# One scheduling priority for every exponential of the scores in a four-layer linear-attention and memory-attention kernel

## The chip, the cores and the metric

The kernel runs on one core of a Trainium2 chip. The metric is the device time of one execution in microseconds (us); the time before is the median of three runs. The engines are named as in the profile: PE is TensorE (PEld its weight loads), DVE is VectorE, ACT is ScalarE, POOL is GpSimd, SP is SyncE, which only issues DMA transfers. L1068 is line 1068 of the kernel.

## The reference

Four layers in the order A, B, A, B on an input of 2048 rows by 640; each adds its result to its input. `H` = 32 heads of 20.

```python
# A: linear attention
qkv = (layernorm(x) @ wqkv) split into q, k, v;  phi(t) = where(t > 0, t + 1, exp(t)) + 1e-6
pq, pk = phi(q), phi(k)
o = (pq @ (pk.T @ v)) / (pq @ sum(pk) + 1e-6);   x = x + o @ wo
# B: memory and local attention over 4 segments of 512 rows
for s in range(4):
    p = softmax(qs @ ks.T * scale + causal mask)
    a_mem = (phi(qs) @ M) / (phi(qs) @ z + 1e-6)          # phi without the 1e-6
    o = sigmoid(beta) * a_mem + (1 - sigmoid(beta)) * (p @ vs)
    M, z = M + phi(ks).T @ vs, z + sum(phi(ks))
x = x + concat(o) @ wo
```

## The kernel before

**Two streams.** The kernel is written as two generators. The *dense* stream holds all projections, the layernorms, the linear attention of the A layers, and the memory and output of the B layers. The *attention* stream holds the causal softmax of the two B layers. `run` weaves them: it steps the stream that has the smaller estimated cost so far. What comes out is the written order. TensorE takes its instructions exactly in that order (`manual_schedule` for PE). For ScalarE, VectorE, GpSimd and SyncE a scheduler decides when the kernel is built: of the instructions that it takes to be ready it picks by priority, which is the place in the written order, moved forward by `tc.high_priority(offset=n)` for what is written inside that block. Once built, each engine's order is fixed.

**Attention.** A B layer has 4 segments of 8 groups of 4 heads, so there are 64 groups in all. Each goes through `attention` in three stretches (the table `STRETCHES`; the third number of an entry says how many groups back it works, so that three groups are under way at a time):

- `row_max`: scores with the queries as rows (TensorE, L1023) and their row maxima (VectorE, L1029); `split_max` (VectorE, L1038 and L1039) and `max_rows` (L1047 to L1052) turn the maxima into two more rows of the queries.
- `scores`: the scores again, transposed, with the maximum taken off by the matmul (L1064) into one PSUM bank; the exponential by ScalarE (L1068) into a tile `pe`, of which there are ten; the selection of the causal part of a diagonal block by GpSimd (L1075). A group has ten banks, written as five pairs by `EXPS[0]` to `EXPS[4]`: 640 exponentials and 640 selections.
- `weigh` (TensorE, L1091) multiplies the exponentials by the values, `evacuate` (ScalarE, L1097) and `normalize` (L1104 to L1115) finish the group.

**PSUM.** All PSUM tiles come from one pool of eight banks. Which instruction reads a bank last (an exponential, or one of the dense instructions below) decides when TensorE may write into it again; the banks are handed on in the order in which they come free.

**Dense instructions near the exponentials.** `turn` (L325 to L339) transposes a 128-row tile by TensorE (L332) in two parts of three and two chunks; ScalarE writes the upper half of each number, in 16 bits (L336), and VectorE the lower half from that (L337). The projection that reads both, `proj_n`, issues for each of the five chunks three matmuls (L415): upper by upper, upper by the weight's lower half, and lower by upper. `proj_t` (L400) does the same for queries and keys, whose result goes through `split_store` (L853 by ScalarE, L854 by VectorE, then a store). `phi` (B layers: L439 exponential `e`, L441 relu `r`, both ScalarE, L442 VectorE) and `phi_a` (A layers: L429, L431, L432) make phi, reading the same PSUM bank twice. In B layers L442 makes `pkT`, which TensorE turns (L881) and ScalarE writes out (L883) for `update`: L891 TensorE, L897 VectorE, which adds to `acc`; at a segment's end the memory `mem` is added up by VectorE (L750). `normed` (L387, ScalarE) makes a layernorm's row `xh`. `o_half` writes half of an output tile (L491 ScalarE, L492 GpSimd), and `b_out` stores it (L990, issued by ScalarE).

Of the kernel before, what the change touches and what calls it, by code (L numbers as in the profile page):

```python
# [144 lines left out]
class Kernel:  # L145
# [974 lines left out]
    def attention(self, segs):  # L1120

        prev = old = ahead = None
        n = 0
        while n < NSEG * NG or prev or old:
            new = None
            if n < NSEG * NG:
                st = segs[n // NG]
                if not st.get("projected"):
                    yield lambda: st.get("projected")
                new = ahead or self.stacks(st, n % NG)  # L1130
                ahead = None
            n += 1
            for stretch in STRETCHES:
                for op, k, back in stretch:
                    G = (new, prev, old)[back]
                    if op == "load" and n < NSEG * NG and segs[n // NG].get("projected"):
                        if prev:
                            with self.tc.issue_after(self.rowed.ins):
                                ahead = self.stacks(segs[n // NG], n % NG)
                        else:  # L1140
                            ahead = self.stacks(segs[n // NG], n % NG)
                    if G is None:
                        continue
                    if op == "max":
                        self.row_max(G, MAXES[k])
                    elif op == "split":
                        self.split_max(G)
                    elif op == "rows":
                        self.max_rows(G)
                    elif op == "exp":  # L1150
                        with self.tc.high_priority(offset=200) if k == 4 else nullcontext():
                            for bank in EXPS[k]:
                                self.scores(G, bank)
                    elif op == "sum":
                        self.weigh(G, k)
                    elif op == "copy":
                        self.evacuate(G)
                    elif op == "out":
                        if not G["st"].get("remembered"):
                            yield lambda: G["st"].get("remembered")  # L1160
                        self.normalize(G)
                yield SLOT
            old, prev = prev, new
# [244 lines left out]
```

## Time and profile before

| | |
|---|---|
| Three runs, median (lowest to highest) | 1684.12 us (1683.84 to 1685.31) |
| Profiled execution: time, span | 1683.68 us, 1681.9 us |
| Time outside the span | 1.78 us |
| Granted TensorE clock, mean | 0.997 |
| TensorE busy (weight loads) | 1625.1 us (1018.3 us) |
| VectorE, ScalarE, GpSimd busy | 1262.9, 994.8, 505.5 us |
| First and last exponential of scores | 363.7 us, 1654.2 us |

The span is the time from the first to the last instruction of the profiled execution. A timeline's line gives the start, the length, the engine, the line in the kernel, what it writes and reads, how many instructions it stands for ("x4"), and in brackets how long the engine stood idle before it and what ended that. Starts and lengths of several instructions on one line are those of the first start and the total. In a view of who waits, a line gives the engine and line that waited or was waited for, the microseconds, and the number of times.

### The profile page before, as it was taken

How to read it: one execution, taken by the hardware profiler on the slowest of the kernel's cores; microseconds unless marked ns; L12 is line 12 of the kernel's file. 1: busy time of each engine (PE TensorE's matmuls, PEld its weight loads, DVE VectorE, ACT ScalarE, POOL GpSimd, SP SyncE). 2: the span in 40 equal slices, each digit the busy share in tenths (PEclk: the TensorE clock that was granted, in tenths of full speed). 3: DMA queues.
4: the chain of work that ended last, by engine and by line, in shares of the span. 5: the costliest groups of instructions: out<-in, count | busy, mean ns of one | idle time of the engine just before them, and what ended most of it. 6: DMA issues, size and time to landing. Idle time of an engine off the chain costs nothing.

```text
span 1681.9 us, 37873 instructions
## 1 busy us (share of the span) xinstructions
PE 1625.1 (97%) x13818; PEld 1018.3 (61%) x13818; DVE 1262.9 (75%) x4015; ACT 994.8 (59%) x1888; POOL 505.5 (30%) x1046
## 2 busy tenths in 40 slices
PE   8999998999999999999999999999999999999999
PEld 6767766564475566556556777765546645645555
DVE  6788796397887788759874465947888888878773
ACT  5665553346757746667666464333675676676674
POOL 3442141113223332333351210310322332232452
PEclk9999999999999999999999999999999999999999
DMA  6415546331322332362211303534233323323432
GB/s 221 149 56 192 215 168 205 124 113 58 113 80 70 117 127 67 125 194 75 84 45 41 118 32 108 185 100 135 68 109 102 107 88 111 112 84 104 143 102 95
DMA packets 110514, 190.98 MB, mean 114 GB/s; under 512 B 14188, under 2 KB 69868, under 8 KB 107768
## 3 DMA queue, kind: packets, MB, share of 16 engines
q1 hardware_dynamic: 97704, 142.68, 26.3%
q0 software_dynamic: 3264, 24.91, 4.2%
q10 hardware_dynamic: 9360, 20.98, 3.2%
q8 instruction: 109, 1.79, 0.4%
q14 instruction: 77, 0.63, 0.1%
HBM read 109.32 MB, written 78.64 MB: 112 GB/s over the span
## 4 chain that ended last, share of the span: by engine, by line
PE 72%; DVE 14%; ACT 8%; DMA 3%; issue 2%; SPq 1%; POOL 1%; ACTq 0%; DVEq 0%; POOLq 0%
PE ps L415 30%; PE ps L400 13%; PE ps L1091 8%; PE ps L591 5%; PE ps L1064 4%; PE ps L332 4%; PE ps L1023 3%; ACT pe L1068 3%; DVE ps L1029 2%; PE ps L468 2%; PE ps L1104 1%; DVE e L432 1%; DVE wmx L245 1%; DVE nat L854 1%; DVE pk L554 1%
## 5 line engine op out<-in xcount | busy, mean ns | idle before, releaser
L1029 DVE CUSTOM_DVE_ANT_0 ps<-ps,maskw 128x384 f32<-128x384 f32 (+3 forms) x1024 | 472.7, 520 | 32.3 <-PE ps L1023 28.1
L1068 ACT ACTIVATE pe<-ps,lsc 128x512 f32<-128x512 f32 x640 | 394.8, 695 | 83.3 <-PE ps L1064 67.9
L1075 POOL TENSOR_SCALAR_AFFINE_SELECT pe<-pe 128x256 f32<-128x256 f32 (+1 forms) x640 | 230.9, 367 | 397.6 <-ACT pe L1068 394.4
L415 PEld LDWEIGHTS <-xT 128*128 128x128 f16 x2880 | 280.7, 98 | 110.5 <-issue 4.5
L415 PEld LDWEIGHTS <-oT 128*128 128x128 f16 x1920 | 185.3, 98 | 87.3 <-issue 7.8
L1091 PE MATMUL ps<-pe,v 128*32 128x512 f32 (+3 forms) x2048 | 157.2, 436 | 9.8 <-POOL pe L1075 3.3
L415 PE MATMUL ps<-wm,oT 128*128 128x320 f16 x960 | 142.7, 301 | 4.8 <-DVE oT L337 4.4
L415 PE MATMUL ps<-w_Bo,oT 128*128 128x320 f16 x960 | 141.5, 299 | 3.8 <-ACT oT L336 2.0
L1029 DVE DVE_READ_ACCUMULATOR2_ANT mg<- 128x1 f32 x1024 | 143.8, 140 | 0.1
L591 PE MATMUL ps<-pk,xs 128*128 128x321 f16 (+1 forms) x960 | 139.0, 302 | 5.0 <-DVE pk L554 2.4
L400 PE MATMUL ps<-xT,w_Bq 128*128 128x512 f16 x600 | 140.9, 380 | 1.3 <-ACT pe L1068 0.8
L415 PE MATMUL ps<-w_Ak,xT 128*128 128x320 f16 x960 | 139.7, 301 | 1.6 <-DVE xT L337 0.9
L400 PE MATMUL ps<-xT,w_Bk 128*128 128x512 f16 x600 | 138.5, 379 | 1.2 <-ACT pe L1068 1.2
L415 PE MATMUL ps<-w_Bv,xT 128*128 128x320 f16 x960 | 139.3, 299 | 0.1
L415 PE MATMUL ps<-w_Aq,xT 128*128 128x320 f16 x960 | 137.6, 299 | 0.0
L1064 PE MATMUL ps<-qs,ks 62*128 62x512 f16 (+3 forms) x1024 | 129.5, 299 | 3.6 <-ACT pe L1068 2.2
L591 PEld LDWEIGHTS <-xs 128*128 128x128 f16 x960 | 93.4, 98 | 44.9 <-DVE pk L554 2.8
L1023 PE MATMUL ps<-ks,qs 60*128 60x512 f16 (+3 forms) x1024 | 115.8, 297 | 2.3 <-ACT pe L1068 1.1
L432 DVE SCALAR_TENSOR_TENSOR e<-e,r 128x320 f32<-128x320 f32 x128 | 68.2, 534 | 63.7 <-ACT r L431 63.1
L854 DVE SCALAR_TENSOR_TENSOR nat<-ps,nat 128x512 f16<-128x512 f32 x80 | 55.2, 690 | 66.2 <-ACT nat L853 65.8
L1091 PEld LDWEIGHTS ps<-pe,v 128*32 128x32 f32 x2048 | 63.2, 109 | 68.9 <-issue 47.3
L336 ACT ACTIVATE oT<-ps 128x384 f16<-128x384 f32 (+1 forms) x128 | 55.9, 445 | 71.7 <-PE ps L332 54.3
(202 smaller groups left out, 2369.0 us busy)
## 6 DMA issues: line engine op xcount, KB each, us to landing
x<-xn ACTq DMA_DIRECT2D x48, 320.0 KB
qs<-qd SPq DMA_DIRECT2D x128, 120.0 KB
ks<-kd SPq DMA_DIRECT2D x128, 120.0 KB
xo<-x SPq DMA_DIRECT2D x48, 320.0 KB
pqi<-pqd SPq DMA_DIRECT2D x32, 320.0 KB
qd<-nat SPq DMA_DIRECT2D x40, 256.0 KB
kd<-nat SPq DMA_DIRECT2D x40, 256.0 KB
x<-in_A_x SPq DMA_DIRECT2D x16, 320.0 KB
```

What stands on the lines that cost most here:

```text
L332: nc.tensor.transpose(pt[:, (c - c0) * P:(c - c0 + 1) * P], src[:, c * P:(c + 1) * P], self.ident)
L400: nc.tensor.matmul(p, w[:, c, a, t * P:(t + 1) * P], xT[:, c, b, :], start=k == 0, stop=k == 3 * C - 1)
L415: nc.tensor.matmul(p, xT[:, c, a, i * P:(i + 1) * P], w[:, c, b, n * HN:(n + 1) * HN], start=k == 0, stop=k == 3 * C - 1)
L432: nc.vector.scalar_tensor_tensor(e, e, 1.0, r, op0=OP.min, op1=OP.add)
L591: nc.tensor.matmul(p, xs[:, i, a, c * P:(c + 1) * P], pk[i][:, b, cols], start=i == 0 and a == b, stop=i == NT - 1 and a == 1)
L854: nc.vector.scalar_tensor_tensor(nat[:, 1], p, QK_SHIFT, nat[:, 0], op0=OP.mult, op1=OP.subtract)
L1023: nc.tensor.matmul(bs[par][:, a:a + n], qs[r, p, i * P:(i + 1) * P], ks[r, p, :n], start=True, stop=True)
L1029: nc.vector.tensor_tensor_reduce(bs[par][:, a:a + n], bs[par][:, a:a + n], self.maskw[:, SEG - n:], 1.0, NEG, OP.add, OP.max, G["mg"][:, p ...
L1064: nc.tensor.matmul(b[:, a:a + n], ks[r, p, j * P:(j + 1) * P], qs[r, p, j * P:], start=True, stop=True)
L1068: nc.scalar.activation(e, b, AF.Exp, scale=self.lsc)
L1075: nc.gpsimd.affine_select(d, d, pattern=pat, compare_op=OP.is_ge, fill=0.0, base=0, channel_multiplier=-1)
L1091: nc.tensor.matmul(G["pv"][32 * h4:32 * h4 + 32, j * P:], v[j][:, h * E1:h * E1 + 32], G.pop((p, par, j)), start=j == 0, stop=j == 2, skip ...
```

## The change

Before, only the last pair of a group (`EXPS[4]`) was written at a priority 200 places ahead, and the other four pairs at none. Now these four have a priority 100 places ahead; the last pair keeps its 200. The block holds all of `scores`: on TensorE it decides nothing (that order is the written one), on ScalarE and GpSimd it moves exponentials and selections against the dense instructions.

```diff
                     elif op == "exp":
-                        with self.tc.high_priority(offset=200) if k == 4 else nullcontext():
+                        with self.tc.high_priority(offset=200 if k == 4 else 100):
                             for bank in EXPS[k]:
                                 self.scores(G, bank)
```

No instruction is added or removed. The orders of TensorE and SyncE are the same before and after. On ScalarE 90 of the 640 exponentials stand earlier, in 32 places, each time ahead of one or two dense instructions: 12 places (25 exponentials) pass e and r of `phi` (L439, L441), 8 (24) pass `xh` (L387), 7 (25) pass r of `phi_a` (L431, at some also L567), 2 (5) pass L491, 2 (8) pass L336, and 1 (3) passes the issue of a store (L990). On GpSimd nine selections stand earlier. On VectorE, which has no instruction inside the block, some 27 dense instructions stand later, because what they read now comes later.

Three places follow. First ScalarE near the end, in the last segment of the last B layer (1625 us in the trace of before). `oT` are the halves that the output projection reads, `xn` an output row. Before:

```order
L491 ACTIVATE xn<-ps,ioB 128x320
L1068 ACTIVATE pe<-ps,lsc 128x512
L990 DMA out_x<-xn 128x640
L1068 ACTIVATE pe<-ps,lsc 128x512 x3
L336 ACTIVATE oT<-ps 128x3x128
L336 ACTIVATE oT<-ps 128x2x128
L1068 ACTIVATE pe<-ps,lsc 128x512 x4
L336 ACTIVATE oT<-ps 128x3x128
L491 ACTIVATE xn<-ps,ioB 128x320
```

Now:

```order
L491 ACTIVATE xn<-ps,ioB 128x320
L1068 ACTIVATE pe<-ps,lsc 128x512
L990 DMA out_x<-xn 128x640
L1068 ACTIVATE pe<-ps,lsc 128x512 x7
L336 ACTIVATE oT<-ps 128x3x128
L336 ACTIVATE oT<-ps 128x2x128
L336 ACTIVATE oT<-ps 128x3x128
L491 ACTIVATE xn<-ps,ioB 128x320
```

The four exponentials that followed the first two `oT` instructions now stand before them.

Second VectorE at the end of the second B layer's third segment (1403 us). `pkT` is phi of the keys, `m_19613` the split row maxima, `mem_80` the segment's memory. Before:

```order
L897 TENSOR_TENSOR acc<-ps,acc 128x63
L442 SCALAR_TENSOR_TENSOR pkT<-e,r 128x512
L1038 TENSOR_SCALAR m_19613<-mg 128x2x8
L750 TENSOR_TENSOR mem_80<-acc,blk 32x3x63
L1039 SCALAR_TENSOR_TENSOR m_19613<-mg,m_19613 128x2x8
L750 TENSOR_TENSOR mem_80<-acc,blk 32x3x63 x2
L750 TENSOR_TENSOR mem_80<-acc,blk 32x63
L854 SCALAR_TENSOR_TENSOR nat<-ps,nat 128x512
```

Now:

```order
L897 TENSOR_TENSOR acc<-ps,acc 128x63
L1038 TENSOR_SCALAR m_19613<-mg 128x2x8
L750 TENSOR_TENSOR mem_80<-acc,blk 32x3x63
L1039 SCALAR_TENSOR_TENSOR m_19613<-mg,m_19613 128x2x8
L750 TENSOR_TENSOR mem_80<-acc,blk 32x3x63 x2
L750 TENSOR_TENSOR mem_80<-acc,blk 32x63
L442 SCALAR_TENSOR_TENSOR pkT<-e,r 128x512
L854 SCALAR_TENSOR_TENSOR nat<-ps,nat 128x512
```

`pkT` now stands behind the maxima's split and the memory. (On ScalarE at this place, its e and r stand behind two exponentials that followed them.)

Third ScalarE in the first B layer, where `phi_a` of the next A layer's queries is made (783 us). Numbers behind names tell tiles apart. Before:

```order
L336 ACTIVATE oT_10927<-ps_10928 128x3x128
L429 ACTIVATE e_10950<-ps_10934,inv_Aq_601 128x320
L431 ACTIVATE r_10952<-ps_10934,inv_Aq_601 128x320
L1068 ACTIVATE pe_10960<-ps_10957,lsc_2933 128x512
L1068 ACTIVATE pe_10966<-ps_10963,lsc_2933 128x512
L1068 ACTIVATE pe_10985<-ps_10982,lsc_2933 128x512
L1068 ACTIVATE pe_10991<-ps_10988,lsc_2933 128x512
L336 ACTIVATE oT_10927<-ps_11000 128x2x128
```

Now:

```order
L336 ACTIVATE oT_10927<-ps_10928 128x3x128
L429 ACTIVATE e_10950<-ps_10934,inv_Aq_601 128x320
L1068 ACTIVATE pe_10960<-ps_10957,lsc_2933 128x512
L1068 ACTIVATE pe_10966<-ps_10963,lsc_2933 128x512
L1068 ACTIVATE pe_10985<-ps_10982,lsc_2933 128x512
L1068 ACTIVATE pe_10991<-ps_10988,lsc_2933 128x512
L431 ACTIVATE r_10952<-ps_10934,inv_Aq_601 128x320
L336 ACTIVATE oT_10927<-ps_11000 128x2x128
```

`r_10952`, the second reader of the bank `ps_10934`, now stands behind four exponentials.

## The prediction

> **What bounds the kernel now.** I read the page first, then the groups by line, then everything that stands around the exponentials (L1068), then the timeline wherever the change moves one.
>
> ```profile
> span 1681.9 us, 37873 instructions
> PE 1625.1 (97%) x13818; PEld 1018.3 (61%) x13818; DVE 1262.9 (75%) x4015; ACT 994.8 (59%) x1888; POOL 505.5 (30%) x1046
> PE 72%; DVE 14%; ACT 8%; DMA 3%; issue 2%; SPq 1%; POOL 1%; ACTq 0%; DVEq 0%; POOLq 0%
> L1068 ACT ACTIVATE pe<-ps,lsc 128x512 f32<-128x512 f32 x640 | 394.8, 695 | 83.3 <-PE ps L1064 67.9
> ```
>
> TensorE is busy for 1625.1 of 1681.9 us, and its order is the written one, which the change leaves alone. So only the 56.8 us in which it stands can shrink, and whatever makes it stand longer adds. ScalarE is busy 59% of the span: it is no bound, but it serves TensorE in turn, and the change alters whose turn comes first. One exponential has 695 ns. Who waits for exponentials is told by the view of line 1068:
>
> ```profile
>   POOL pe L1075: 394.4, 429
>   PE ps L1091: 2.4, 6
>   PE ps L891: 2.4, 6
>   PE ps L1064: 2.2, 6
>   PE ps L400: 2.0, 5
>   PE ps L1023: 1.1, 3
>   PE ps L415: 0.6, 2
>   PE ps L332: 0.6, 2
> ```
>
> GpSimd waits for them for 394.4 us, but it is busy 30% of the time and bounds nothing. TensorE waits 2.4+2.4+2.2+2.0+1.1+0.6+0.6 = 11.3 us, in 30 instances, for all 640. Nearly all are waits for a PSUM bank (all eight are in one pool, so the exponential that reads a bank frees it for whatever TensorE does next). 11.3 us is therefore all that earlier exponentials could ever bring, if nothing else became later.
>
> **What the change moves.** TensorE's and SyncE's orders stay. On ScalarE 90 of the 640 exponentials, in 32 places, go ahead of one or two dense instructions; on GpSimd nine selections move; on VectorE some 27 dense instructions slip behind maxima and memory updates. No instruction is added or removed. So the cost is that of the passed dense instructions, place by place: what each feeds, and when that is wanted.
>
> *The oT halves, two places.* The first is in the last B segment, at 1625 us:
>
> ```profile
> 1625.19 0.77 ACT L336 ACTIVATE oT<-ps 128x384 f16<-128x384 f32 x2
> 1625.36 0.37 PE L1064 MATMUL ps<-qs,ks 62*128 62x384 f16 x2 [0.20 <-ACT pe L1068]
> 1625.72 0.89 DVE L337 TENSOR_TENSOR oT<-ps,oT 128x384 f16<-128x384 f32 x2
> 1625.82 2.45 ACT L1068 ACTIVATE pe<-ps,lsc 128x512 f32<-128x512 f32 x4
> 1626.42 0.52 PE L332 MATMUL ps<-ident,otok 128*128 128x128 f32 x3 [0.69 <-DVE oT L337]
> 1626.78 2.20 PE L415 MATMUL ps<-w_Bo,oT 128*128 128x320 f16 x15
> 1628.10 0.55 ACT L336 ACTIVATE oT<-ps 128x384 f16<-128x384 f32 x1
> 1628.74 0.56 DVE L337 TENSOR_TENSOR oT<-ps,oT 128x384 f16<-128x384 f32 x1 [0.85 <-ACT oT L336]
> ```
>
> Here ScalarE makes the upper halves of oT (L336), VectorE the lower ones (L337), and the output projection (L415) reads both: its third matmul is the first that needs a lower half. The four exponentials now run first. Their slot is 2.28 us (1625.82 to the next instruction at 1628.10), and their scores are done by 1625.36+0.37 = 1625.73 at the latest, in time for the third and fourth. So the first L336 starts at 1625.19+2.28 = 1627.47 and not at 1625.19. VectorE follows 0.53 behind its start (1625.72 against 1625.19) and takes 0.56: the lower half is there at 1628.56, and with 0.06 for the handover the third matmul starts at 1628.62. Before, it started two steps of 2.20/15 = 0.147 after 1626.78, at 1627.07. That is **+1.55 us**. Bounds: no less than 0 (it would have to be absorbed by a later wait), no more than the whole slot, 2.28. The L332 before it waited 0.69 for VectorE to free a bank and now gets one from the first exponential, but the projection behind it still waits, so this brings nothing.
>
> The second such place is at 1573.86, and what it turns is read by the projection that begins here:
>
> ```profile
> 1579.89 0.31 PE L415 MATMUL ps<-w_Bo,oT 128*128 128x320 f16 x1
> ```
>
> A delay of 2.28 us disappears in the six before that. Without that cover it would cost as much as the first.
>
> *e and r in front of pkT, 12 places, 25 exponentials* (L439, L441). The two are pushed back by two exponentials, 1.14 us. In eleven places what they feed is wanted later. The twelfth is the segment's last tile:
>
> ```profile
> 1402.27 0.70 ACT L439 ACTIVATE e<-ps,inv_Bk 128x512 f32<-128x512 f32 x1
> 1403.36 0.22 DVE L897 TENSOR_TENSOR acc<-ps,acc 128x63 f32<-128x63 f32 x1
> 1403.41 1.29 ACT L1068 ACTIVATE pe<-ps,lsc 128x512 f32<-128x512 f32 x2
> 1403.58 0.69 DVE L442 SCALAR_TENSOR_TENSOR pkT<-e,r 128x512 f32<-128x512 f32 x1
> 1404.19 0.17 DVE L1038 TENSOR_SCALAR m<-mg 128x16 f16<-128x16 f32 x1
> 1404.90 1.13 DVE L750 TENSOR_TENSOR mem<-acc,blk 32x189 f32<-32x189 f32 x3
> 1405.12 0.60 PE L881 MATMUL ps<-ident,pkT 128*128 128x128 f32 x4
> ```
>
> The push of 1.14 is the distance of ScalarE's starts, 1402.27 to 1403.41. VectorE pays more than that, since pkT's place in its order is now behind L1038, L1039 and all of L750. Those last from 1404.19 to 1404.90+1.13 = 1406.03, 1.84 us; begun at 1403.58 they end at 1405.42, and pkT at 1406.11 instead of 1404.27. The transposes L881 began at 1405.12, behind TensorE's own earlier work, and now begin at about 1406.16: **+1.04 us**. Least: 0.3, if VectorE took pkT as soon as r is there (1403.58+1.14+0.69 = 1405.41). Most: 1.84, if TensorE had been held to pkT already. For the other eleven I take 0, because what frees the last bank of the group is finished when all four instructions are, in either order:
>
> ```profile
> 540.14 0.75 ACT L441 ACTIVATE r<-ps,inv_Bq 128x512 f32<-128x512 f32 x1
> 542.19 0.64 PE L1091 MATMUL ps<-pe,v 128*32 128x512 f32 x4 [0.30 <-ACT pe L1068]
> ```
>
> Here the matmul waited 0.30 for the last exponential and will wait as long for r. Bounds: 0.75 against 0.695 a place, +0.6 in all; or this 0.30 gone wherever it stands, which the gains below hold.
>
> *r of the linear layers, seven places, 25 exponentials* (L431):
>
> ```profile
> 782.94 0.38 PE L1064 MATMUL ps<-qs,ks 62*128 62x384 f16 x4
> 783.02 0.52 ACT L431 ACTIVATE r<-ps,inv_Aq 128x320 f32<-128x320 f32 x1
> 783.43 2.42 ACT L1068 ACTIVATE pe<-ps,lsc 128x512 f32<-128x512 f32 x4
> 783.59 2.20 PE L415 MATMUL ps<-w_Ak,xT 128*128 128x320 f16 x15
> ```
>
> At 783.59 TensorE starts as r ends (783.54) and frees its bank. Now an exponential stands there, which takes 0.695 and not 0.52: +0.17. Five of the seven have this shape: **+0.85 us** (0 to 1.2, seven places). r itself is four exponentials late, 2.28 us; it goes through VectorE into a store whose result no matmul of this stretch reads. If it were read at once, seven places would cost 16 us.
>
> *xh of the layernorm, eight places, 24 exponentials* (L387):
>
> ```profile
> 476.27 0.91 ACT L387 ACTIVATE xh<-xn,nb,rs 128x640 f32<-128x640 f32 x1
> 489.57 0.60 PE L332 MATMUL ps<-ident,xh 128*128 128x128 f32 x4
> ```
>
> xh comes three exponentials later, 3 x 0.57 = 1.7 us, and is turned 12 us after it was made: 0. Without that cover it would be 1.7 each, 14 us. The last three places (L491 twice, an output store once) pass work with no reader near: 0.
>
> *Gains.* The 90 moved exponentials end sooner. If the 11.3 us were spread evenly over 640, those outside the e/r places (65) would hold 65/640 x 11.3 = 1.1; the timeline shows some waits of 0.1 to 0.2 at them, and I take **-1.0 us** (bounds 0 and 90/640 x 11.3 = 1.6).
>
> Sum: 1.55+1.04+0.85-1.0 = **+2.4 us**. The profiled execution took 1683.68 us, 0.44 below the median of 1684.12, and 1.78 outside its span. The edit touches nothing outside the span, so 1683.68 becomes 1686.1, and the median 1686.5.
>
> **A rule against the change.** ScalarE's own waits for scores are in the list of waits:
>
> ```profile
> ACT pe L1068 <- PE ps L1064: 67.9, 80, 3.5
> ```
>
> Eighty of the 640 exponentials stood on ScalarE until their scores came, 67.9/80 = 0.85 us each, 3.5 the longest. Whatever stands behind such a one waits too, and a moved exponential has ready dense work behind it. At the places above the scores end before the slot (1625.73 for the last one at 1625; at 783 the slot is 783.02, and the matmuls of the second pair begin at 782.94, so the first pair is through), so my sum holds nothing for it. [...]
>
> **Rivals.** *Slower: the moved exponential blocks.* If the 32 places met unfinished scores as often as the rest (80 of 640), four would, for 0.85 each: 3.4 us on top, if TensorE waits behind each. That is 1686.5+3.4 = 1689.9; with the two holes at their upper bounds alone (0.73 and 0.8 more) 1688.0. It decides once 1.0 us is added to my sum, so from two such places. Against it: where I followed the scores, they were done. Chance 0.22.
>
> *Slower: the clock.* The two holes widen TensorE's idle time, and the granted clock is not full in every stretch (columns: TensorE busy first, the clock is the third value from the right):
>
> ```profile
> 240.00:300.00 60.00, 54.37 (x436) 38.32 (x434) 42.77 (x107) 21.67 (x50) 14.70 (x18) 0.97 0.51 176
> 1620.00:1680.00 60.00, 56.47 (x477) 36.05 (x475) 27.95 (x89) 30.90 (x60) 20.50 (x42) 1.00 0.30 100
> ```
>
> With 5.6 us idle in 60 the clock was 0.97; with 3.5 us it was 1.00. The last stretch gets 1.55 more, 5.1, close to the former. Price: 0.03 x 60 = 1.8 us, 1688.3. [...] No row here shows the step itself. Chance 0.06.
>
> *No change: nothing shows.* 550 exponentials stay where they were, and the holes may be taken up by waits that follow them. Then only small gains and losses remain: 1684.1, at the lowest 1684.12-1.6 = 1682.5. Against it: TensorE stood only 3.5 us in the last 60, mostly for its own results. Chance 0.14.
>
> *Faster: freed banks run ahead.* Thirty waits for exponentials against 32 places. If half the 11.3 us went and no hole appeared, 1684.1-5.6 = 1678.5. It would decide from 3.4 us on. Against it: the places are where the scheduler had a choice, not where TensorE waited, and the 0.30 above doesn't go. Chance 0.08.
>
> **The numbers.** The forecast has 0.50, from 1685.1 to 1687.4. 0.2% is 3.4 us, about what a measurement can tell from no change: 1680.7 to 1687.5. Same: forecast and no change, 0.64; slower: 0.22+0.06 = 0.28; faster 0.08. The range goes from the lowest of the no-change case, 1682.5, to 1689.5, and leaves out the faster case and the top of the first rival, some 0.15.
>
> **What would show it.** Right: at about 1626.4 TensorE stands some 1.6 us ahead of an L415 released by VectorE's L337; at about 1405 some 1.0 us ahead of L881, released by L442; its busy time stays 1625; its waits for L1068 stay between 9 and 12 us. Wrong: neither hole there, an L1068 in front of which ScalarE idles at a moved place while TensorE stands, waits for L1068 below 8, or a clock under 1.00 in the last 60 us.

## The result, and the profile after

| | before | after |
|---|---|---|
| Median of 20 runs each (lowest to highest) | 1683.78 us (1680.32 to 1686.06) | 1685.83 us (1683.27 to 1688.28) |
| Ratio of the runs, 95% interval | | 1.0015 (1.0009 to 1.0022) |
| Profiled execution: time, span | 1683.68, 1681.9 us | 1685.54, 1683.8 us |
| Granted TensorE clock in it | 0.997 | 0.995 |

The change costs 1.5 to 3.7 us. The page of the profile after:

```profile
span 1683.8 us, 37888 instructions
PE 1625.1 (97%) x13818; PEld 1018.1 (60%) x13818; DVE 1260.8 (75%) x4015; ACT 995.1 (59%) x1888; POOL 503.6 (30%) x1046
```

TensorE's busy time has the same sum as before, 1625.1 us, but differences offset in it: with its instructions matched one to one (below), it is busy 3.1 us longer from 1624 us on, most of that at half clock, 1.5 us shorter ahead of the first exponential of scores, and 1.6 us shorter between. So the 1.9 us of the span can't be read as waiting alone. Who waits for exponentials, from the view of line 1068 after:

```profile
  PE ps L1064: 2.8, 7
  PE ps L891: 2.4, 6
  PE ps L1091: 2.2, 3
  PE ps L400: 2.0, 5
  PE ps L1023: 1.1, 3
  PE ps L332: 0.8, 3
  PE ps L415: 0.6, 2
```

That is 11.9 us where it was 11.3: ninety exponentials earlier, and TensorE waits for exponentials no less. What it waits for otherwise is seen at the two places of the prediction. The timeline after, at 1625 us:

```profile
1625.16 1.19 ACT L336 ACTIVATE oT<-ps 128x384 f16<-128x384 f32 x3
1625.72 1.35 DVE L337 TENSOR_TENSOR oT<-ps,oT 128x384 f16<-128x384 f32 x3 [1.01 <-ACT oT L336]
1625.75 4.24 PE L415 MATMUL ps<-w_Bo,oT 128*128 128x320 f16 x15 [1.57 <-ACT oT L336]
1629.92 0.61 PE L1064 MATMUL ps<-qs,ks 62*128 62x256 f16 x4
```

The projection stands 1.57 us for oT's upper half. But then its fifteen matmuls take 4.24 us, where they took 2.20 before. The stretches of the same kernel show why (the clock is the third value from the right):

```profile
1624.00:1626.00 2.00, 0.43 (x4) 0.13 (x2) 0.92 (x5) 2.00 (x6) 1.33 (x4) 0.58 0.05 17
1626.00:1628.00 2.00, 2.00 (x9) 0.97 (x8) 1.08 (x3) 0.35 (x1) 0.00 (x0) 0.50 0.00 0
1628.00:1630.00 2.00, 2.00 (x10) 0.91 (x10) 0.00 (x0) 0.00 (x0) 0.00 (x0) 0.50 0.00 0
1630.00:1632.00 2.00, 2.00 (x18) 0.80 (x22) 1.01 (x3) 1.79 (x3) 1.22 (x2) 0.71 0.00 0
1620.00:1680.00 60.00, 56.79 (x458) 35.00 (x455) 26.22 (x83) 30.49 (x59) 20.28 (x42) 0.94 0.27 91
```

The clock of 0.58 in the first row means half speed from about 1624.3 on, while TensorE stands (1624.18 to 1625.75); the trace's records of the clock put the spell at 1624.32 to 1631.15. So behind the wait TensorE works at half speed for 5.4 us; over the 60 us the clock is 0.94, where it was 1.00. The other place, after:

```profile
1403.67 0.69 DVE L442 SCALAR_TENSOR_TENSOR pkT<-e,r 128x512 f32<-128x512 f32 x1
1404.42 0.66 PE L881 MATMUL ps<-ident,pkT 128*128 128x128 f32 x4 [0.76 <-DVE pkT L442]
```

L881 had no wait before and has 0.76 now, for VectorE's L442, as forecast (some 1.0).

Since TensorE's order is the same in both kernels, its instructions can be matched one to one, and the difference of their starts (after less before) tells where time was lost. Up to the first exponential both kernels are the same; that one started 1.2 us sooner in the profile after, by chance (over the profiles shown below this start scatters by 2 us to either side). Counted from there, in us:

| stretch of before | step | what is there |
|---|---|---|
| 364 to 782 | -0.35 | several small ones |
| 782 to 833 | +0.24 | r places (L431) |
| 833 to 850 | +0.47 | L1091 waits 1.40, not 0.70 |
| 862 to 868 | -0.85 | L591 no longer waits for L611 |
| 868 to 1395 | +0.07 | |
| 1395 to 1409 | +0.97 | L881 waits for L442 |
| 1558 to 1564 | -0.99 | the issue of a store is short |
| 1588 to 1592 | -0.56 | L415 waits 0.24, not 0.81, for L336 |
| 1624 to 1631 | +3.89 | the wait for oT and the half clock |
| 1631 to the end | +0.28 | |

The rest of -0.1 lies between 1409 and 1558; the sum is +3.06. What makes the +0.28 behind 1631 was not followed.

### The profile page after: what moved, and what is told of

Same layout as the page of the kernel before. It is cut to its first block, busy times and chain, and to the rows that moved or that the text cites. A ratio compares the mean times of both kernels' runs of the same rounds, so it can differ in the third digit from the quotient of the medians.

```text
span 1683.8 us, 37888 instructions
## 1 busy us (share of the span) xinstructions
PE 1625.1 (97%) x13818; PEld 1018.1 (60%) x13818; DVE 1260.8 (75%) x4015; ACT 995.1 (59%) x1888; POOL 503.6 (30%) x1046
## 4 chain that ended last, share of the span: by engine, by line
PE 72%; DVE 14%; ACT 7%; DMA 3%; issue 2%; SPq 1%; POOL 1%; ACTq 0%; DVEq 0%; POOLq 0%
PE ps L415 30%; PE ps L400 13%; PE ps L1091 8%; PE ps L591 5%; PE ps L1064 4%; PE ps L332 4%; PE ps L1023 3%; ACT pe L1068 3%; DVE ps L1029 2%; PE ps L468 2%; PE ps L1104 1%; DVE e L432 1%; DVE wmx L245 1%; DVE pk L554 1%; DVE nat L854 1%
## 5 line engine op out<-in xcount | busy, mean ns | idle before, releaser
L1068 ACT ACTIVATE pe<-ps,lsc 128x512 f32<-128x512 f32 x640 | 393.3, 694 | 82.7 <-PE ps L1064 69.0
L415 PEld LDWEIGHTS <-xT 128*128 128x128 f16 x2880 | 280.9, 98 | 111.3 <-issue 4.9
L415 PEld LDWEIGHTS <-oT 128*128 128x128 f16 x1920 | 185.7, 98 | 89.7 <-DVE oT L337 8.1
L1091 PE MATMUL ps<-pe,v 128*32 128x512 f32 (+3 forms) x2048 | 157.7, 436 | 12.2 <-ACT r L441 3.7
L415 PE MATMUL ps<-w_Bo,oT 128*128 128x320 f16 x960 | 143.6, 302 | 4.7 <-ACT oT L336 3.0
L415 PE MATMUL ps<-wm,oT 128*128 128x320 f16 x960 | 142.7, 301 | 5.1 <-DVE oT L337 4.8
L415 PE MATMUL ps<-w_Ak,xT 128*128 128x320 f16 x960 | 140.4, 302 | 1.6 <-DVE xT L337 1.0
L591 PE MATMUL ps<-pk,xs 128*128 128x321 f16 (+1 forms) x960 | 137.1, 300 | 3.6 <-DVE pk L554 2.2
L415 PE MATMUL ps<-w_Bv,xT 128*128 128x320 f16 x960 | 139.3, 299 | 0.1
L415 PE MATMUL ps<-w_Aq,xT 128*128 128x320 f16 x960 | 137.6, 299 | 0.1
L591 PEld LDWEIGHTS <-xs 128*128 128x128 f16 x960 | 92.7, 97 | 42.4 <-DVE pk L554 2.7
L1091 PEld LDWEIGHTS ps<-pe,v 128*32 128x32 f32 x2048 | 62.8, 109 | 72.2 <-issue 50.5
L400 PEld LDWEIGHTS <-w_Bk 128*128 128x128 f16 x600 | 57.0, 98 | 67.3 <-issue 7.1
```

Of the source, the lines that this page charges most:

```text
L400: nc.tensor.matmul(p, w[:, c, a, t * P:(t + 1) * P], xT[:, c, b, :], start=k == 0, stop=k == 3 * C - 1)
L415: nc.tensor.matmul(p, xT[:, c, a, i * P:(i + 1) * P], w[:, c, b, n * HN:(n + 1) * HN], start=k == 0, stop=k == 3 * C - 1)
L591: nc.tensor.matmul(p, xs[:, i, a, c * P:(c + 1) * P], pk[i][:, b, cols], start=i == 0 and a == b, stop=i == NT - 1 and a == 1)
L1068: nc.scalar.activation(e, b, AF.Exp, scale=self.lsc)
L1091: nc.tensor.matmul(G["pv"][32 * h4:32 * h4 + 32, j * P:], v[j][:, h * E1:h * E1 + 32], G.pop((p, par, j)), start=j == 0, stop=j == 2, skip ...
```

## The experiments

The first three ask whether the place at 1625 carries the cost, and whether the clock falls because of the wait there. In `attention`, a pair is named by the B layer, segment and group at hand, and k. The changed kernel without the priority at this one place:

```diff
-                        with self.tc.high_priority(offset=200 if k == 4 else 100):
+                        with self.tc.high_priority(offset=200 if k == 4 else 100) if k == 4 or (self.jobs.index(segs), G["st"]["s"], G["g"], k) not in ((1, 3, 5, 2), (1, 3, 5, 3)) else nullcontext():
```

> The change everywhere but at one place: the four exponentials near 1625 us get no priority and stand behind the two L336 again, as before the change. Theory (the wait there costs 1.4 us, and the half clock that follows it another 2.4 in most executions): about 3.3 us less than the changed kernel, 0.9 us under the kernel before (1682.9, ratio 0.9995); clock 1.00 over 1620 to 1680 and no wait of over 1 us ahead of that L415. Rival 1 (the fall of the clock has nothing to do with this wait): 1.5 us less than the changed kernel, 0.9 over the kernel before, and the clock still 0.94 in that stretch. Rival 2 (the cost is spread over all 32 places): 4 of 90 exponentials are worth 0.1 us, so 2.3 over the kernel before.

Measured: median 1684.41 us of 11 runs, the kernel before beside it 1683.50; ratio 1.0000 (0.9991 to 1.0009). The wait is gone and with it the difference from the kernel before, as far as these runs can tell. But the theory was too simple, and the expected gain of 0.9 didn't come: in its profile the clock is not 1.00 here.

```profile
1627.55 3.27 PE L415 MATMUL ps<-w_Bo,oT 128*128 128x320 f16 x15
1620.00:1680.00 60.00, 57.87 (x477) 36.80 (x475) 27.87 (x88) 31.21 (x61) 20.49 (x42) 0.97 0.29 97
```

A half-speed spell of 3.4 us falls on this place in this execution with the order of before. So the place can lose the clock without the long wait.

The kernel before with the priority at this place alone (the same edit with `in` for `not in`):

> The kernel before, with the priority added at this one place alone (four exponentials of 640). Theory: 2.5 to 3.9 us over the kernel before (1687.1, ratio 1.0020), with the wait of about 1.5 us ahead of L415 and a clock of 0.94 to 0.96 over 1620 to 1680. Rival 1: 1.5 over, clock 1.00 there. Rival 2: 0.1 over.

Measured: 1685.81 us, ratio 1.0014 (1.0005 to 1.0023). Four exponentials of 640 cost as much as the whole change. (0.3 us of that lie outside its span, 2.07 on average where the other kernels have 1.7 to 1.8.) Its profile:

```profile
1627.67 3.86 PE L415 MATMUL ps<-w_Bo,oT 128*128 128x320 f16 x15 [1.57 <-ACT oT L336]
1620.00:1680.00 60.00, 56.64 (x466) 35.40 (x464) 27.05 (x86) 31.01 (x60) 20.52 (x42) 0.97 0.29 97
```

The same wait of 1.57, and one half-speed spell, where the changed kernel's profile has two in a row: the clock is 0.97 where 0.94 to 0.96 were expected, and the cost 2.3 us where 2.5 to 3.9 were. Rival 2, a cost spread over the 32 places, is out.

The changed kernel with the wait filled by work. In `proj_n`, for this one projection:

```diff
-            p = self.bank()[:, :HN]
+            p = self.bank()[:, :HN]; [nc.tensor.matmul(p[:, :P], self.ident, self.ident, start=True, stop=True) for _ in range(self.fill)]; self.fill = 0
```

with `self.fill` 7 there and 0 elsewhere (the trace counts fourteen matmuls for these seven).

> The changed kernel, with seven matmuls of the identity by itself put into TensorE's order ahead of the L415 that waits near 1625 us; they write the bank that the projection's first matmul overwrites, so they fill the wait and change nothing else. Theory (an idle TensorE lowers the clock): the L415 starts as late as in the changed kernel, within 0.3 us, but the clock stays 1.00 over 1620 to 1680, and the time falls by 2.0 to 2.4 us, to 0 to 0.5 over the kernel before. Rival 1: clock 0.94 as in the changed kernel, and its time, 2.3 over the kernel before. Rival 3 (work costs the same as waiting, the clock is lost for other reasons such as power): slower than the changed kernel.

Measured: 1684.11 us, ratio 1.0003 (0.9994 to 1.0012). The profile, timeline and stretch:

```profile
1627.15 1.73 PE L411 MATMUL ps<-ident 128*128 128x128 f32 x14
1628.30 1.19 ACT L336 ACTIVATE oT<-ps 128x384 f16<-128x384 f32 x3
1628.88 2.53 PE L415 MATMUL ps<-w_Bo,oT 128*128 128x320 f16 x15
1620.00:1680.00 60.00, 58.20 (x489) 37.33 (x488) 28.21 (x91) 31.54 (x61) 20.43 (x42) 1.00 0.29 97
```

The projection starts just as late after its L336 (0.58 behind, 0.59 in the changed kernel), yet its matmuls take 2.53 and the clock is 1.00. Doing useless work in the wait brings 1.7 us by the medians (1685.83 to 1684.11) of runs taken at different times, whose ratios to before just overlap (from 1.0009 and up to 1.0012). That speaks against rivals 1 and 3. The difference of starts at this place is +1.60 here, at full clock: that is the wait by itself.

All twelve profiles shown in this document can be compared at this place. In each, all half-speed spells begin on one raster of 3.41 us: by the trace's records of the clock at 28.21, 116.96 and 260.32 us in the kernel before (26 and 42 times 3.413 apart), at 26.88, 258.99 and 1624.32 in the changed one (68 and 400 times). The table has how long TensorE stood in each stretch of that raster near 1625 us, by what followed the stretch, and what the place costs by the difference of starts from 1624 to 1631:

| order at 1625 | idle us, then half speed | idle us, then full speed | cost, us |
|---|---|---|---|
| changed (five profiles) | 1.05 and 1.43; 1.93; 1.81; 1.99; 1.54 | up to 0.71 | 3.9; 3.2; 2.9; 3.2; 2.7 |
| of before (five) | 0.83; 1.29 | up to 0.89 | 1.4; 1.6; 0; 0; 0 |
| changed and filled (two) | none | up to 0.53 | 1.6; 1.6 |

The first figures of the first row are the changed kernel's own profile. Its first spell begins when only 0.14 of the 1.57 us of waiting have passed, so the shorter waits ahead of it (1.05 in the stretch before) stand ahead of that spell, and the long wait (1.43) ahead of the second. In the other four the long wait, or most of it, lies in the stretch before their one spell. With the wait every unfilled profile has a spell, without it two of five, filled neither: the wait makes a spell likelier, and the changed kernel's profile, with two, is the costliest of its kind. How long TensorE stood isn't the whole of it: in the changed kernel a stretch with 1.40 idle at 832 us has full clock behind it. What else counts is open.

The place at 1403, undone alone (the first edit with `!= (1, 1, 6, 3)`):

> The change everywhere but at the place near 1403 us: two exponentials get no priority, so e, r and pkT keep their old places on ScalarE and VectorE. Theory (L881's wait there costs 0.9 us): 0.9 us less than the changed kernel, 1.4 over the kernel before, and no wait ahead of L881. Rival 2 (spread): less than 0.1 us from the changed kernel. Rival 4 (the wait at 1405 is given back before the end, since later waits become shorter): the wait goes, the time stays.

Measured: 1684.77 us, ratio 1.0007 (0.9999 to 1.0016), 1.1 less than the changed kernel's median in its own runs. Its profile has no wait ahead of L881:

```profile
1402.66 0.69 DVE L442 SCALAR_TENSOR_TENSOR pkT<-e,r 128x512 f32<-128x512 f32 x1
1404.21 0.60 PE L881 MATMUL ps<-ident,pkT 128*128 128x128 f32 x4
```

The step from 1395 to 1409 is 0.00 instead of +0.97, and nothing later takes it back, against rival 4.

Both places undone:

> The change everywhere but at both places: neither the four exponentials near 1625 us nor the two near 1403 us get the priority; the other 84 moved exponentials keep it. Theory (the two waits and the clock carry the cost, the rest of the change is a small gain): both waits gone, 0.9 us less than without the one place at 1625 alone, so 1683.1 to 1683.5 against 1683.5 of the kernel before; mean granted clock about 0.9963, as there. Rival 2 (the cost is spread over the 32 places): 1 to 2 us over the kernel before.

Measured: 1681.74 us, the kernel before beside it 1683.21; ratio 0.9989 (0.9980 to 0.9998). With two of the 32 places taken out, the kernel is 0.3 to 3.4 us faster than before. By the difference of starts it gains 2.08 in its profile, of which 0.99 lie at a store's issue where nothing was moved (below); the rest is about the 1.0 us that I gave the gains.

The filled wait, with 1403 undone too:

> The changed kernel with the wait near 1625 us filled by seven matmuls whose result is overwritten, and without the priority at the place near 1403 us. Theory: the clock as in the kernel that is only filled (mean 0.9967), the wait at 1405 gone, 0.9 us less than that kernel: 1683.2 to 1683.4, 0.1 to 0.3 under the kernel before, the fastest of all that keep the change at 1625. Rival 4 (the wait at 1405 is given back): 1684.2, as the one that is only filled.

Measured: 1682.46 us, ratio 0.9994 (0.9985 to 1.0003). From 1592 to 1629 its starts move by +1.61 at full clock. It is the fastest of those that keep the change at 1625, as expected, and the wait at 1403 stays saved. By the medians, not to wait (both undone) is better still than to fill the wait; the intervals overlap.

The next one is about the step of -0.99 at 1558, where nothing was moved. Before, and after:

```profile
1558.44 2.85 ACTq L990 DMA_DIRECT2D out_x<-xn  x1
1562.30 0.44 PE L332 MATMUL ps<-ident,ol 128*128 128x128 f32 x2 [0.92 <-ACT xn L491]
```

```profile
1557.68 0.37 ACTq L990 DMA_DIRECT2D out_x<-xn  x1
1560.56 0.44 PE L332 MATMUL ps<-ident,ol 128*128 128x128 f32 x2
```

ScalarE's issue of the store takes 2.85 us before; L336 and L491 stand behind it, and TensorE waits 0.92. In the same stretch (1556 to 1563) the transfers of before hold a load of instructions on queue 14, which those of after do not:

```profile
q14 instruction: 1, 0.01, 0.3%
```

The kernel before with ScalarE's instructions pushed 16 places on, at about 350 us:

```diff
-        self.open_b(L)
+        self.open_b(L); z = self.cp.tile([1, 16], F32, name="nil"); [self.nc.scalar.activation(z[:, j:j + 1], wB["o"][:1, 0, 0, :1], AF.Copy) for j in range(16)]
```

> The kernel before, with 16 activations of one number each on ScalarE at about 350 us, whose result nothing reads; all else in its order. They push every later instruction of ScalarE 16 places on in its stream. Theory (the issue of a store at 1558 us that takes 2.85 us in the kernel before and 0.37 in the changed one stands behind a load of ScalarE's instructions, and it is chance of place which kernel has it): that issue falls under 0.5 us, TensorE runs 1.0 us earlier from 1564 on, and the time falls by about 1.0 us, to 1682.5. Rival 5 (it is a property of that store, the first to the output, or of the order around it, which the change improves): the issue takes 2.8 to 3.1 us again and the time stays at 1683.5.

Measured: the issue takes 0.38 us, and TensorE is 0.99 us earlier from 1564 on:

```profile
1556.73 0.38 ACTq L990 DMA_DIRECT2D out_x<-xn  x1
1559.60 0.44 PE L332 MATMUL ps<-ident,ol 128*128 128x128 f32 x2
```

The time is 1683.01 us, ratio 0.9998 (0.9989 to 1.0006): the interval holds the 1.0 us, but does not show it. In this execution the 0.99 was lost again near 1625, where a half-speed spell cost 1.6 with the order of before. So 1.0 us of what the change gained in its profile is not the priority's doing; in this one profile, moving ScalarE's instructions by 16 places was enough for it. In all profiles the long issue and the load on queue 14 go together (the kernel before and the one with 1625 alone have both, 3.06 us in the latter; the rest have neither). That the load is ScalarE's is argued, not shown.

The place at 831, undone alone (exponentials that pass r of L431):

> The change everywhere but at one place of the linear layers near 831 us: four exponentials there don't pass r (L431), so L567 (the upper halves of phi of the keys, on ScalarE) gets its input as early as before. Theory (ScalarE stands at L567 for the late r, and the group's last exponentials stand behind it, so the matmul L1091 waits 1.40 us instead of 0.70 at 834): the wait is back at 0.70, and TensorE is 0.4 to 0.5 us earlier at 850; by 900 this is lost again, since the wait of 0.80 us ahead of L591 at 866 that the change removed is partly back. Rival 6 (the loss stands to the end): 0.4 us earlier at 900 too, relative to the first exponential.

Measured, one execution: 1684.86 us. L1091 in the changed kernel and in this one:

```profile
832.47 0.56 ACT L567 ACTIVATE pk<-e,k_scl 128x320 f16<-128x320 f32 x1 [0.56 <-DVE e L432]
834.17 1.07 PE L1091 MATMUL ps<-pe,v 128*32 128x512 f32 x8 [1.40 <-ACT pe L1068]
```

```profile
834.10 1.07 PE L1091 MATMUL ps<-pe,v 128*32 128x512 f32 x8 [0.69 <-ACT pe L1068]
```

As expected the wait halves. But it isn't given back: between 364 and 900 this kernel gains 1.18 us on before, where the changed one gains 0.54. That part of the theory falls, and rival 6 holds: the place costs 0.6 us up to 900, of which 0.5 are left at 1558. In the changed kernel ScalarE stands 0.56 at L567, whose input comes through VectorE from the late r, and the group's last exponentials stand behind L567. An early exponential has made a late one.

All three undone:

> The change everywhere but at three places: near 1625, 1403 and 831 us, where it made TensorE wait longer. Theory: the wait ahead of L1091 at 834 is 0.70 again beside the two others being gone, so 0.5 to 0.6 us less than without the two alone: 1681.1 to 1681.6 where the kernel before has 1683.2, ratio about 0.9988. Rival 2 (the cost is spread over the 32 places): 1 us over the kernel before.

Measured: 1681.74 us, the kernel before beside it 1683.26; ratio 0.9992 (0.9983 to 1.0001). The wait ahead of L1091 is 0.69, but the 0.6 us don't show against the kernel with two undone, which stood at the same median. By the starts its lead over that kernel is 0.68 at 900, 0.18 at 1558, and gone at the end (a gain of 2.01 on before against 2.08), lost in small steps near 904, 1480 and 1642. So whether this place costs time at the end is open.

And the gains: the changed kernel without the priority near 863 and near 1587.

> The changed kernel without the priority at two places where it brought time: one exponential near 863 us (it passes L491, and with it VectorE's order of L611 and L369 turns round) and three near 1587 us (they pass the issue of a store, L990). Theory (these two are worth 0.9 and 0.6 us): L591 waits 0.8 us for L611 again and TensorE is 0.8 to 0.9 us later from 866 on than in the changed kernel, by its distance from the first exponential; L415 at 1590 waits 0.8 for L336 again, 0.5 to 0.6 us later from there on. Rival 7 (they come from other moved exponentials or from the store's shorter issue at 1558): no difference at either place.

Measured, one execution: 1686.55 us. VectorE and TensorE at 865, in the kernel before, in the changed one, and in this one:

```profile
864.82 0.49 DVE L369 BATCH_NORM_STATS2 st<-xn 128x6 f32<-128x320 f32 x1 [3.00 <-POOL xn L492]
865.23 0.48 DVE L611 COPY v<-ps 128x321 f32<-128x321 f32 x1
865.76 1.53 PE L591 MATMUL ps<-pk,xs 128*128 128x321 f16 x10 [0.80 <-DVE v L611]
```

```profile
861.35 0.49 DVE L611 COPY v<-ps 128x321 f32<-128x321 f32 x1 [0.37 <-PE ps L591]
864.05 1.68 PE L591 MATMUL ps<-pk,xs 128*128 128x321 f16 x11
```

```profile
865.17 0.47 DVE L611 COPY v<-ps 128x321 f32<-128x321 f32 x1
865.70 1.80 PE L591 MATMUL ps<-pk,xs 128*128 128x321 f16 x12 [0.71 <-DVE v L611]
```

With the priority gone, L611 is back behind L369, which waits three microseconds for GpSimd, and L591 waits again: the step of -0.85 from 862 to 868 becomes -0.09, and that from 1564 to 1592 +0.01 instead of -0.56. Two moved places bring 1.3 us, and at neither does TensorE wait for an exponential.

## Why the prediction was right, and where not

The forecast was 1686.5 us, 2.4 above the median known then; measured are 1685.83 and, against the 20 runs of before, +2.05 by medians or +2.5 by the ratio. The sign, the size and the two places are as forecast. Of the signs named, the waits for L1068 came (11.9), and the hole ahead of L881. The hole near 1625 is released by L336 and not by L337, and a sign of being wrong came too: a clock under 1.00 in the last 60 us. Term by term:

- **The wait for oT**, 1.55 forecast: 1.60 with the clock kept full. The steps of that term hold: the four exponentials' slot, then L336, then L337, then the third matmul, which in the filled kernel starts 1.60 later than before. The 1.57 that the trace shows stand ahead of the first matmul, which needs only L336.
- **pkT behind L750**, 1.04 forecast: 0.97. In the changed kernel VectorE begins L1038 and L750 sooner, but TensorE too comes there sooner.
- **r places**, 0.85 forecast: about 0.2 at the five named (782 to 833: 0.24), so the longer exponential in r's stead is mostly hidden. The 0.6 at 834 lies at one of these places, but by another way: "it goes through VectorE into a store whose result no matmul of this stretch reads" was true of the queries. For the keys r also feeds L567 on ScalarE itself, and exponentials stand behind that one. That step of the prediction was wrong.
- **The gains**, 1.0 forecast: 0.35 up to 782, 0.85 at 866, 0.56 at 1590, and 0.99 at 1558, 2.75 in all. The step that failed is the bound: I counted only waits for exponentials as what could be gained (at most 1.6). The two that the experiments turned off are waits for dense work: a moved exponential let VectorE take L611 ahead of an instruction that stands, and let L336 go sooner after the issue of a store. The 0.99 isn't the priority's at all.
- **The clock**, nothing forecast, and a chance of 0.06: it came. In the profiled execution it costs 3.89-1.60 = 2.3 us; in the four other profiles with the long wait 1.1 to 1.6. Over the runs the mean granted clock is 0.9950 for the changed kernel (20 runs) and 0.9965 for the kernel before (33 runs taken beside the experiments): 0.0015 x 1683 = 2.5 us of full speed, of which some falls on waiting. Beside the same 33 runs the kernel with the place at 1625 alone has 0.9957, which makes 0.0008 x 1683 = 1.3. With 1625 filled it is 0.9967, with 1625 undone 0.9963.

So the number came out by luck, through two errors that offset each other: gains too small by 1.75, and the clock left out, 2.3 in that execution and 1.1 to 2.5 by the other figures. Of the rivals, "the clock" was priced rightly for one spell (1.8) and held far too unlikely: its 0.06 was an estimate of mine that rested on no run. I had read idle time per 60 us; the spells followed what lay within a few microseconds. Near 1625 the half clock came behind stretches of 3.41 us in which TensorE stood 0.83 to 1.99 us in all, and no single wait among them was longer than 1.57. Why a spell comes in some executions and not in others with the same order at this place (two of five with that of before) was not shown. The first rival, an exponential with unfinished scores at the head of ScalarE's queue, did not come in that form. In the trace after, none of the 88 moved exponentials that a comparison of the two orders finds has ScalarE standing idle in front of it, and over all 640 ScalarE waited 67.9 us for scores before and hardly more after:

```profile
ACT pe L1068 <- PE ps L1064: 69.0, 79, 3.7
```

What blocked instead were dense instructions at the head, L567 on ScalarE (0.56 us, in the changed kernel) and L369 on VectorE (3.00 us, in the kernel before), once for worse and once for better.

## What to carry to other kernels

Where a priority is given to a whole class of instructions, look place by place at what each one passes and who waits for that: here two places of 32 cost 2.6 us plus the clock, and the same change without them is faster than before (0.9989; some 1.0 us of that lies at the store's issue, where no exponential was moved). Ask of each passed instruction not only who reads it, but whether its reader is on the same engine and what stands behind that reader. And look at a new wait of TensorE twice: once for its length, once for the clock behind it, which cost 1.1 to 2.3 us here beside the wait's 1.6; if it can't be removed, work that nobody reads, put into it, kept the clock full in two profiles.

## What the runs showed of the hardware

- The half-speed spells of TensorE (granted clock 0.50) lasted 3.41 us, or twice that: 6.83 from 1624.32 us in the changed kernel's profile. Near 1625 us all five profiles with the changed order have them, two of five with the order of before, and neither of the two with the wait filled. These came behind stretches of 3.41 us with 0.83 to 1.99 us of idle time; but twice 0.89 there, and 1.40 at 832 us in the changed kernel, had none behind them.
- A DMA issue on ScalarE took 2.85 us in the kernel before and 3.06 in the one with 1625 alone, 0.37 in the changed one and 0.38 in the one with 1625 undone, at the same place of the program. With ScalarE's instructions shifted by 16 it took 0.38 in the one profile taken.
- The start-up, the same instructions in nearly all kernels, ends 2.0 us sooner to 1.9 us later than in the profile of before. That is as much as the change itself, so a difference of two single executions says little, and the steps between matched instructions say more.
